# Joining two kinds of small-tile matmul runs, and one subtraction moved from VectorE to GpSimd

## The chip, the cores and the metric

The kernel runs on one core of a Trainium2 chip. The metric is the device time of one execution in microseconds (us). The profile is of one execution on the same chip; its span runs from its first instruction to its last.

## What is computed

The output is the sum of three things over a sequence of 2048 rows of 576 channels: the input itself, a long convolution (a diagonal state-space model, applied by FFT), and a feed-forward block. Both branches take the same layer-normalised input.

```python
def _A_ref(u, A_re, A_im, B_re, B_im, C_re, C_im, log_dt, Dskip):
    dt = jnp.exp(log_dt)[:, None]
    logdA, dB = dt * (A_re + 1j * A_im), dt * (B_re + 1j * B_im)
    P = jnp.exp(logdA[:, :, None] * l[None, None, :])        # l = 0..2047
    K = jnp.einsum("dn,dnl,dn->dl", C_re + 1j * C_im, P, dB).real
    ...
    Yf = rfft(u, padded) * rfft(K, padded)
    y = irfft(Yf)[:, :L] + u * Dskip
def _B_ref(x, w1, w2):
    return silu(x @ w1) @ w2                                 # 576 -> 4608 -> 576
xn = layernorm(A_u)
return A_u + _A_ref(xn, ...) + _B_ref(xn, w1, w2)
```

## The kernel before

**The main stream** is the feed-forward block (`ffn`, lines 257 to 446). It walks over 36 blocks: two halves of the rows, nine chunks of the hidden dimension, two row blocks of 512. `up` (L331 to L333) makes four 128 x 512 tiles `ph` of a chunk's hidden values, `down` (L357) multiplies them with the second weights into `po` tiles of 128 x 288, and VectorE adds each into the accumulator `acc` (L361). All matmuls are in a three-term form: every operand is split into a high and a low part (`gh`, `gl`, `w1h`, `w1l` and so on), ScalarE (ACT) making the high one and VectorE (DVE) the low one by a subtraction.

**The side stream** (`side`, from L863) is the convolution. The generator `weave` (L33) mixes it into the main stream: each `yield` of the side stream names a share of the main stream's steps, and the code up to the next `yield` is issued when the main stream has come that far. The last word on the order has a scheduler, which plans all engines' queues when the program is built; `tc.high_priority()` and `tc.issue_after` (here `behind(ins)`) are its hints. Each engine then runs its own queue strictly in that order. The stage from mark 0.13 to mark 0.597 of the main stream holds two parts:

- `kgen` (L584 to L728) makes the first transform of the convolution kernel K, 8 channels of each of two groups per step, 36 steps. A step makes tables `S` and `C` of 128 x 16 x 96 on DVE and ACT (L653 to L677). Every second step, after two steps' tables (a pair), 64 small matmuls of tile shape 128 x 32 write the response products `kp` (L696; the profile counts 128, since a float32 matmul runs in two passes). ACT copies them to `kt` (L703). Then eight small matmuls of tile shape 64 x 128 apply the first transform, into two PSUM tiles `z` (L711, counted as 16), and ACT copies those into `stage` (L719). Every second pair, two DMAs on SyncE's queue (SP) store `stage` into `d1k` (L724). Behind the loop, a GpSimd DMA adds the skip weights into `d1k` (L727).
- `spread` (L145 to L166) makes the first transform of the inputs, 16 row groups in two halves each, one half per step of `kgen`. A half loads `xr`, ACT casts its 64 rows to the high part in `sp` (L156), the low part is a subtraction of 64 x 576 (L157), four full-size matmuls make two `pu` tiles (L161, L162), ACT copies them to `u1` (L163), and a DMA on GpSimd's queue stores them to `d1u` (L164). The pool `up` has one buffer of each of `xr`, `sp` and `u1`.

`kp`, `z` and `pu` take their PSUM buffers from one pool, `pss`, with three. `po` takes from `ps2` (three), `ph` from `ps1` (two). Then the spectral stage (`spectral`, from L730) reads `d1u` and `d1k`, multiplies the spectra (`pk`, `pu`, `pb`, L826), and stores to `d2`; `add_conv` (L847, small tiles `py`) adds the inverse transform to the output rows.

Of the kernel before, what the change touches and what calls it, by code (L numbers as in the profile page):

```python
# [11 lines left out]
F32 = mybir.dt.float32  # L12
# [7 lines left out]
P = 128  # L20
# [23 lines left out]
def kernel(  # L44
# [21 lines left out]
    nc = tc.nc  # L66
# [14 lines left out]
    d1k = dram.tile([32 * P, D], F32, name="d1k")  # L81
# [9 lines left out]
    f1 = cst.tile([P, P], F32, name="f1")  # L91
# [18 lines left out]
    pss = ctx.enter_context(tc.tile_pool(name="pss", bufs=3, space=PSUM))  # L110
# [31 lines left out]
    def behind(ins):  # L142
        return tc.issue_after(ins) if ins is not None else nullcontext()

    def spread(up):  # L145

        s1 = up.tile([P, 2, P], F32R, name="s1", bufs=1)
        nc.gpsimd.dma_start(s1, cs1)
        for j in range(NJ):
            src = up.tile([P, D], F32, tag="xr", name="xr")  # L150
            nc.sync.dma_start(src, dxn[:, j])
            for m in range(2):
                lo, hi = slice(64 * m, 64 * m + 64), slice(64 - 64 * m, 128 - 64 * m)
                u1 = up.tile([P, D], F32, tag="u1", name="u1")
                sp = up.tile([P, D], F32R, tag="sp", name="sp")
                nc.scalar.copy(sp[lo, :], src[lo, :])  # L156
                nc.vector.tensor_sub(sp[hi, :], src[lo, :], sp[lo, :])  # L157
                for h in range(2):
                    hs = slice(h * HD, (h + 1) * HD)
                    pu = pss.tile([P, 512], F32, tag="pss", name="pu")  # L160
                    nc.tensor.matmul(pu[:, :HD], s1[:, 0, :], sp[:, hs], start=True, stop=False)  # L161
                    nc.tensor.matmul(pu[:, :HD], s1[:, 1, :], sp[:, hs], start=False, stop=True)  # L162
                    nc.scalar.copy(u1[:, hs], pu[:, :HD])  # L163
                nc.gpsimd.dma_start(  # L164
                    d1u.rearrange("(p m j) d -> m j p d", m=2, j=NJ)[m, j], u1)
                yield j  # L166
# [417 lines left out]
    def kgen():  # L584
        fT, phiT = kf["f"], kf["phi"]
        with tc.tile_pool(name="kg", bufs=1) as kg:
            CH = 8
            NRUN = 4
# [46 lines left out]
            def head(i):  # L635
                th = kg.tile([P, W, 65], F32, tag="th", name="th", bufs=2)
                nc.vector.tensor_mul(split(th), row(vt[:, 0:65], 65), col(fT, i, 65))
                with behind(pins["gl"]):
                    nc.vector.tensor_add(split(th)[:, :, :, :32], split(th)[:, :, :, :32], col(phiT, i, 32))
                return th  # L640

            stage = None
            tabs = []
            nxt = head(0)
            al = powers(0)
            for i in range(NCK):
                th = nxt
                pk, ak = pw[:, i % 2], al[:, :, i % 2]
                c65 = kg.tile([P, W, 65], F32, tag="c65", name="c65")
                S = kg.tile([P, W, 96], F32, tag="S", name="S", bufs=2)  # L650
                C = kg.tile([P, W, 96], F32, tag="C", name="C", bufs=2)
                mag = C
                nc.scalar.activation(c65, th, AF.Identity, bias=magic)  # L653
                nc.vector.scalar_tensor_tensor(th, c65, MAGIC, th, op0=ALU.subtract, op1=ALU.subtract)  # L654
                nc.scalar.activation(c65, th, AF.Abs)  # L655
                nc.scalar.activation(th, th, AF.Sin, scale=TWO_PI)
                nc.scalar.activation(c65, c65, AF.Sin, scale=-TWO_PI, bias=halfpi)
                for g in range(2):
                    gs = slice(g * CH, (g + 1) * CH)
                    nc.vector.tensor_mul(  # L660
                        mag[:, gs, 0:32].rearrange("n d (x y) -> n d x y", y=4),
                        pk[:, gs, 0, :].unsqueeze(3).broadcast_to([P, CH, 8, 4]),
                        ak[:, g].unsqueeze(2).broadcast_to([P, CH, 8, 4]))
                nc.vector.tensor_mul(
                    mag[:, :, 32:96].rearrange("n d (x y) -> n d x y", y=8),
                    pk[:, :, 1, :].unsqueeze(3).broadcast_to([P, W, 8, 8]),
                    pk[:, :, 2, :].unsqueeze(2).broadcast_to([P, W, 8, 8]))
                if i + 1 < NCK:
                    nxt = head(i + 1)
                    if i % 2 == 1:  # L670
                        al = powers(i + 1)
                for dst, t, sg in ((S, th, -1.0), (C, c65, 1.0)):
                    ov3 = dst.rearrange("n d (x y) -> n d x y", y=32)[:, :, 0:3:2, :]
                    mv3 = mag.rearrange("n d (x y) -> n d x y", y=32)[:, :, 0:3:2, :]
                    nc.vector.tensor_mul(ov3, t[:, :, 0:64].rearrange("n d (x y) -> n d x y", y=32), mv3)
                    nc.vector.scalar_tensor_tensor(dst[:, :, 32:64], t[:, :, 64:32:-1], sg, mag[:, :, 32:64],  # L676
                                                   op0=ALU.mult, op1=ALU.mult)  # L677
                tabs.append((S, C))
                if i % 2 == 0:
                    yield (i + 1) / NCK  # L680
                    continue

                kp = pss.tile([P, 512], F32, tag="pss", name="kp")
                first = None
                for e in (1, 0):
                    S, C = tabs[e]
                    for gl in range(2):
                        for gp_ in range(2):
                            o = e * 256 + (gl * 2 + gp_) * 64
                            for q in range(4):  # L690
                                ch = gp_ * CH + gl * 4 + q
                                dst = kp[32 * q:32 * q + 32, o:o + 64]
                                begins = e == 1 and gl == 0 and gp_ == 0
                                with tc.high_priority(), behind(None if begins else first):
                                    for n, t in enumerate((C, S)):
                                        mm = nc.tensor.matmul(dst, t[:, ch, :32], t[:, ch, 32:],  # L696
                                                              start=begins and n == 0, stop=True,
                                                              tile_position=(0, 32 * q), skip_group_check=True)
                                if begins:
                                    first = mm.ins  # L700
                tabs = []
                kt = kg.tile([P, 512], F32, tag="kt", name="kt")
                nc.scalar.copy(kt, kp)  # L703

                z = [pss.tile([P, 512], F32, tag="pss", name="z") for _ in range(2)]
                first = None
                for eg in range(4):
                    for h in (1, 0):
                        rows = slice(64 * h, 64 * h + 64)
                        with tc.high_priority(), behind(first):  # L710
                            mm = nc.tensor.matmul(z[h][:, eg * P:(eg + 1) * P], kt[rows, eg * P:(eg + 1) * P], f1[rows],  # L711
                                                  start=True, stop=True, tile_position=(64 * h, 0))
                        first = first or mm.ins
                r = (i - 1) % NRUN
                if r == 0:
                    stage = kg.tile([P, 64, NRUN * CH], F32, tag="stage", name="stage")
                sv = stage[:, :, r * CH:(r + 2) * CH].rearrange("p k (e h c) -> p h e k c", h=2, c=2)
                for h in range(2):
                    nc.scalar.copy(sv[:, h], z[h].rearrange("p (e k c) -> p e k c", e=4, c=2))  # L719
                if r == NRUN - 2:  # L720
                    d0 = (i // NRUN) * NRUN * CH
                    kv = d1k.rearrange("(k n) (g d) -> g n k d", n=64, g=2)
                    for gp_ in range(2):
                        nc.sync.dma_start(kv[gp_, :, :, d0:d0 + NRUN * CH], stage[gp_ * 64:(gp_ + 1) * 64])  # L724
                yield (i + 1) / NCK

        nc.gpsimd.dma_start(d1k.rearrange("(k n) d -> n k d", n=P)[0],  # L727
                            dskip.unsqueeze(0).broadcast_to([32, D]), accum_op=ALU.add)  # L728
# [294 lines left out]
```

## Time and profile before

| what | value |
|---|---|
| median of three runs | 1110.31 us (1109.8 to 1110.34) |
| span of the profiled execution | 1108.2 us |
| around the span, against the median | 2.1 us |
| TensorE busy in the span | 1102.2 us (99%) |
| VectorE busy in the span | 916.6 us (83%) |
| ScalarE busy in the span | 706.9 us (64%) |
| GpSimd busy in the span | 72.1 us (7%) |

The profile names engines PE (TensorE matmul), PEld (its weight loads), DVE (VectorE), ACT (ScalarE), POOL (GpSimd) and SP (SyncE). A row of the timeline has the start in us from the span's start, the duration in us, the engine, the line of the kernel, the operation, the tile written and those read, and the shape; "x4" merges four equal ones. A row of groups has the count, the busy time in us, the mean duration in ns, and the idle time ahead of the group with what ended it. A row of windows has the stretch, its length, each engine's busy time with its count of instructions, and at the end the granted clock of TensorE, the DMA engines' share and GB/s. Matmuls are pipelined: their durations overlap, so the distance from start to start is what one costs.

### The profile page before, as it was taken

Reading aid. Unit: us, or ns where it says so; the run is one execution under the profiler, and the core shown is the slowest. Engines: PE = TensorE matmul, PEld = TensorE weight load, DVE = VectorE, ACT = ScalarE, POOL = GpSimd, SP = SyncE. Lnnn points to the kernel's source line nnn. Section 1 sums busy time; section 2 is a strip of 40 time slices with the busy share of each in tenths; the row PEclk is TensorE's granted clock in tenths of the full one; section 3 lists DMA queues with packets and bytes.
Section 4 is the critical chain, followed back from the end, with each engine's and each line's share of the span. In section 5 each row is a group of like instructions: output and inputs, shape, how many; then the busy total and the mean of one; then the engine's idle time right before and its main releaser. Section 6 shows DMA issues by size and latency. Waiting matters only on the chain.

```text
span 1108.2 us, 22917 instructions
## 1 busy us (share of the span) xinstructions
PE 1102.2 (99%) x9167; PEld 997.5 (90%) x9167; DVE 916.6 (83%) x1543; ACT 706.9 (64%) x1222; POOL 72.1 (7%) x129
## 2 busy tenths in 40 slices
PE   9999999999999999999999999999999999999998
PEld 7989998899998899899999989999999999999887
DVE  7799899999999999999999737787778778784433
ACT  4564466676677676677867536877777878774210
POOL 1100000000000000011000000000000000000111
PEclk9999999999999999999999999999999999999999
DMA  9745512525252525264744173554544455434983
GB/s 270 190 123 160 152 50 61 120 73 131 77 121 83 116 72 118 77 174 154 206 122 103 45 179 109 162 167 123 156 145 152 138 149 170 129 107 127 241 224 87
DMA packets 175755, 148.56 MB, mean 134 GB/s; under 512 B 111088, under 2 KB 142592, under 8 KB 175520
## 3 DMA queue, kind: packets, MB, share of 16 engines
q1 hardware_dynamic: 165328, 112.63, 38.7%
q0 software_dynamic: 9568, 33.62, 9.6%
q8 instruction: 72, 1.18, 0.5%
q10 hardware_dynamic: 752, 0.85, 0.3%
q14 instruction: 35, 0.29, 0.1%
HBM read 102.53 MB, written 44.61 MB: 133 GB/s over the span
## 4 chain that ended last, share of the span: by engine, by line
PE 98%; DMA 1%; DVE 1%; SPq 0%; issue 0%; DVEq 0%
PE po L357 42%; PE ph L331 35%; PE kp L696 3%; PE ph L332 3%; PE ph L333 3%; PE pu L826 2%; PE pb L826 2%; PE pk L826 2%; PE z L711 2%; PE pu L161 1%; PE py L847 1%; DMA acc<-in_A_u_dram 1%; PE pu L162 1%; PE pt L124 0%; DVE w1l L295 0%; PE ptk L490 0%
## 5 line engine op out<-in xcount | busy, mean ns | idle before, releaser
L357 PE MATMUL po<-w2l,gh 128*128 128x288 f32 x1152 | 338.5, 295 | 0.0
L357 PE MATMUL po<-w2h,gl 128*128 128x288 f32 x1152 | 336.4, 295 | 0.0
L357 PE MATMUL po<-w2h,gh 128*128 128x288 f32 x1152 | 336.1, 295 | 0.0
L357 PEld LDWEIGHTS po<-w2h,gh 128*128 128x128 f32 x1152 | 215.2, 188 | 7.7 <-issue 2.8
L357 PEld LDWEIGHTS po<-w2l,gh 128*128 128x128 f32 x1152 | 215.9, 188 | 5.1 <-issue 0.5
L357 PEld LDWEIGHTS po<-w2h,gl 128*128 128x128 f32 x1152 | 215.4, 188 | 0.9
L339 ACT ACTIVATE gf<-ph 128x512 f32<-128x512 f32 (+1 forms) x148 | 86.4, 584 | 143.8 <-PE ph L333 134.8
L331 PE MATMUL ph<-xh,w1l 128*128 128x512 f32 (+1 forms) x592 | 161.3, 385 | 0.0
L331 PE MATMUL ph<-xh,w1h 128*128 128x512 f32 (+1 forms) x592 | 161.3, 387 | 0.0
L331 PE MATMUL ph<-xl,w1h 128*128 128x512 f32 (+1 forms) x592 | 161.1, 385 | 0.0
L361 DVE TENSOR_TENSOR acc<-po,acc 128x288 f32<-128x288 f32 x288 | 126.2, 451 | 37.0 <-PE po L357 35.6
L342 DVE TENSOR_TENSOR gl<-gf,gh 128x512 fp32r<-128x512 f32 (+1 forms) x148 | 99.0, 672 | 64.6 <-ACT gh L340 63.8
L331 PEld LDWEIGHTS ph<-xh,w1l 128*128 128x128 f32 x592 | 108.0, 188 | 20.0
L331 PEld LDWEIGHTS ph<-xl,w1h 128*128 128x128 f32 x592 | 107.9, 188 | 19.8
L331 PEld LDWEIGHTS ph<-xh,w1h 128*128 128x128 f32 x592 | 104.5, 188 | 16.7 <-ACT x L133 0.5
L340 ACT CAST gh<-gf 128x512 fp32r<-128x512 f32 (+1 forms) x148 | 89.5, 608 | 9.5 <-PE po L357 6.6
L653 ACT ACTIVATE c<-th,magic 128x1040 f32<-128x1040 f32 x36 | 42.1, 1168 | 37.9 <-DVE C L676 28.0
L655 ACT ACTIVATE c<-th 128x1040 f32<-128x1040 f32 x36 | 38.7, 1075 | 33.6 <-DVE th L654 33.6
L314 ACT CAST w2h<-w2r 128x576 fp32r<-128x576 f32 x72 | 47.0, 671 | 17.7 <-PE po L357 14.9
L295 DVE TENSOR_TENSOR w1l<-w1r,w1h 128x640 fp32r<-128x640 f32 x72 | 56.9, 817 | 0.2
L332 PE MATMUL ph<-x,w1h 128*128 128x512 f32 (+1 forms) x148 | 57.0, 386 | 0.0
L333 PE MATMUL ph<-x,w1l 128*128 128x512 f32 (+1 forms) x148 | 56.9, 385 | 0.0
(185 smaller groups left out, 1828.8 us busy)
## 6 DMA issues: line engine op xcount, KB each, us to landing
w2r<-in_B_w_dram SPq DMA_DIRECT2D x72, 288.0 KB, 3.8
w1r<-in_B_w_dram SPq DMA_DIRECT2D x35, 512.0 KB, 3.8
d1u<-u POOLq DMA_DIRECT2D x32, 288.0 KB, 2.5
d1k<-stage SPq DMA_DIRECT2D x18, 512.0 KB, 6.8
ur<-d1u SPq DMA_DIRECT2D x32, 288.0 KB, 3.7
kr<-d1k SPq DMA_DIRECT2D x32, 288.0 KB, 2.9
d<-yo POOLq DMA_DIRECT2D x32, 288.0 KB, 4.0
ys<-d SPq DMA_DIRECT2D x32, 288.0 KB, 11.8
```

The source lines that it names most:

```text
L295: pins["w1l"] = nc.vector.tensor_sub(l1, src, h1).ins
L314: pins["w2h"] = nc.scalar.copy(h2, r2).ins
L331: nc.tensor.matmul(ph, w[:, kt, :], v[:, kt, a:e], start=n + kt == 0, stop=False)
L332: nc.tensor.matmul(ph, h1[:, 4, :], x4[:, a:e], start=False, stop=False)
L333: pins["pe"] = nc.tensor.matmul(ph, l1[:, 4, :], x4[:, a:e], start=False, stop=True).ins
L339: nc.scalar.activation(gf, ph, AF.Silu)
L340: pins["gh"] = nc.scalar.copy(gh, gf).ins
L342: pins["gl"] = nc.vector.tensor_sub(gl, gf, gh).ins
L357: pins["pe"] = nc.tensor.matmul(po[:, :HD], G[blk, t][g][:, js], W2[half, c, t][w][:, hs], start=n == 0, stop=n == 3 * FT - 1).ins
L361: nc.vector.tensor_add(acc[j][:, hs], po[:, :HD], acc[j][:, hs])
L653: nc.scalar.activation(c65, th, AF.Identity, bias=magic)
L826: nc.tensor.matmul(dst, st, mv[:, hs], start=n == 0, stop=n == 3 * len(terms) - 1)
```

## The change

Two edits. The eight matmuls of the first transform of K, with what follows them (the ACT copies into `stage` and the store into `d1k`), become a function `turn`, which is called one pair late: the response products of a pair are issued, then `turn` for the pair before, whose first matmul is to stand behind the last response product. `kt` gets two buffers for that. The last pair's `turn` is called behind the loop. And the subtraction for the low part of `sp` is issued on GpSimd.

```diff
-                nc.vector.tensor_sub(sp[hi, :], src[lo, :], sp[lo, :])
+                nc.gpsimd.tensor_sub(sp[hi, :], src[lo, :], sp[lo, :])
...
+            stages = []
+            def turn(kt, i, first):
+                z = [pss.tile([P, 512], F32, tag="pss", name="z") for _ in range(2)]
+                for eg in range(4):
+                    for h in (1, 0):
+                        rows = slice(64 * h, 64 * h + 64)
+                        with tc.high_priority(), behind(first):
+                            mm = nc.tensor.matmul(z[h][:, eg * P:(eg + 1) * P], kt[rows, eg * P:(eg + 1) * P], f1[rows],
+                                                  start=True, stop=True, tile_position=(64 * h, 0))
+                        if eg + 1 - h == 0:
+                            first = mm.ins
...
+                for h in range(2):
+                    nc.scalar.copy(sv[:, h], z[h].rearrange("p (e k c) -> p e k c", e=4, c=2))
+                if r == NRUN - 2:
...
+                        nc.sync.dma_start(kv[gp_, :, :, d0:d0 + NRUN * CH], stage[gp_ * 64:(gp_ + 1) * 64])
...
+                                last = mm.ins
...
                 tabs = []
-                kt = kg.tile([P, 512], F32, tag="kt", name="kt")
+                if whole is not None:
+                    turn(*whole, last)
+                kt = kg.tile([P, 512], F32, tag="kt", name="kt", bufs=2)
                 nc.scalar.copy(kt, kp)
-                z = [pss.tile([P, 512], F32, tag="pss", name="z") for _ in range(2)]
...
+                whole = kt, i
                 yield (i + 1) / NCK
+            turn(*whole, None)
```

More of the change, by code (lines that the diff above doesn't have):

```diff
@@ L640, in head @@
                 return th
-            stage = None
+            stages = []
[9 more added lines that the diff above has]
+                            first = mm.ins
+                r = (i - 1) % NRUN
+                if r == 0:
+                    stages.append(kg.tile([P, 64, NRUN * CH], F32, tag="stage", name="stage"))
+                stage = stages[-1]
+                sv = stage[:, :, r * CH:(r + 2) * CH].rearrange("p k (e h c) -> p h e k c", h=2, c=2)
+                for h in range(2):
+                    nc.scalar.copy(sv[:, h], z[h].rearrange("p (e k c) -> p e k c", e=4, c=2))
+                if r == NRUN - 2:
+                    d0 = (i // NRUN) * NRUN * CH
+                    kv = d1k.rearrange("(k n) (g d) -> g n k d", n=64, g=2)
+                    for gp_ in range(2):
+                        nc.sync.dma_start(kv[gp_, :, :, d0:d0 + NRUN * CH], stage[gp_ * 64:(gp_ + 1) * 64])
+            whole = None
             tabs = []
@@ L683, in kgen @@
                 kp = pss.tile([P, 512], F32, tag="pss", name="kp")
-                first = None
+                last = None
                 for e in (1, 0):
@@ L701, in kgen @@
                 tabs = []
-                kt = kg.tile([P, 512], F32, tag="kt", name="kt")
+                if whole is not None:
+                    turn(*whole, last)
+                kt = kg.tile([P, 512], F32, tag="kt", name="kt", bufs=2)
                 nc.scalar.copy(kt, kp)
-                z = [pss.tile([P, 512], F32, tag="pss", name="z") for _ in range(2)]
[L706 to L724, printed above, removed]
+                whole = kt, i
                 yield (i + 1) / NCK
+            turn(*whole, None)
         nc.gpsimd.dma_start(d1k.rearrange("(k n) d -> n k d", n=P)[0],
```

## The prediction

> **What bounds the kernel now.** I read the page's engine sums first, then the chain that ended last, then the stage of the change by windows.
>
> ```profile
> span 1108.2 us, 22917 instructions
> PE 1102.2 (99%) x9167; PEld 997.5 (90%) x9167; DVE 916.6 (83%) x1543; ACT 706.9 (64%) x1222; POOL 72.1 (7%) x129
> PE 98%; DMA 1%; DVE 1%; SPq 0%; issue 0%; DVEq 0%
> ```
>
> The span is TensorE (PE) from end to end: 1102.2 of 1108.2 us busy, and 98% of the chain. So the time changes in two ways only: PE spends fewer or more nanoseconds on its own list, or it is made to wait. The list itself is the same in both programs (the built orders hold equal counts of every instruction; only 32 subtractions go from VectorE, DVE, to GpSimd, POOL). The span is one profiled execution; the median of the three timed runs is 1110.31 us, 2.1 us above it, and I carry differences from one to the other.
>
> Both parts of the change lie in the middle of the span, in the kernel and first-transform stage. There the second engine matters too:
>
> ```profile
> 160.00:610.00 450.00, 437.50 (x654) 1.00 0.42 111
> 200.00:300.00 100.00, 97.64 (x148) 1.00 0.39 102
> 300.00:400.00 100.00, 98.85 (x148) 1.00 0.40 101
> 400.00:500.00 100.00, 95.49 (x143) 1.00 0.44 115
> 500.00:600.00 100.00, 98.24 (x149) 1.00 0.52 143
> 160.00:610.00 450.00, 450.00 (x4694) 406.37 (x4694) 437.50 (x654) 315.49 (x477) 20.44 (x37) 1.00 0.42 111
> ```
>
> The first five rows are DVE's busy time in stretches of the stage, the last has PE, PEld, DVE, ACT, POOL. PE has no idle nanosecond in 450 us, at full granted clock (1.00), and DVE is idle only 12.5 us of them. PE is the bound, but DVE stands a step behind it, and POOL is empty.
>
> **Part 1: the runs of small tiles.** What PE pays at the border between full-size and small-tile matmuls is seen in start times (first number of a row, us), here of one response run's end (kp), then of one transform run's begin and end (z):
>
> ```profile
> 197.18 0.22 PE L696 MATMUL kp<-S 128*32 128x64 f32 x1
> 197.33 0.40 PE L357 MATMUL po<-w2l,gh 128*128 128x288 f32 x1
> 197.57 0.29 PE L357 MATMUL po<-w2h,gl 128*128 128x288 f32 x1
> 197.70 0.29 PE L357 MATMUL po<-w2h,gh 128*128 128x288 f32 x1
> ...
> 202.58 0.39 PE L332 MATMUL ph<-x,w1h 128*128 128x512 f32 x1
> 202.81 0.39 PE L333 MATMUL ph<-x,w1l 128*128 128x512 f32 x1
> 203.13 0.38 PE L711 MATMUL z<-f,kt 64*128 64x128 f32 x2
> ...
> 204.01 0.27 PE L711 MATMUL z<-f,kt 64*128 64x128 f32 x1
> 204.22 0.40 PE L161 MATMUL pu<-sp,s 128*128 128x288 f32 x1
> 204.46 0.30 PE L162 MATMUL pu<-sp,s 128*128 128x288 f32 x1
> 204.59 0.39 PE L331 MATMUL ph<-xh,w1h 128*128 128x512 f32 x1
> ```
>
> Two full-size matmuls follow each other after 0.13 us (288 columns: 197.57 to 197.70) or 0.23 us (512 columns: 202.58 to 202.81). Going into z, the 512-column one is followed after 0.32 us: 0.09 extra. Coming out of kp, 0.15 us pass, where small ones follow each other after about 0.01; then the first full-size one takes 0.24 in place of 0.13: 0.11 extra, a weight load that hides behind no matmul. Out of z it is the same, 0.21 us and then 0.24.
>
> Before: 18 kp runs and 18 z runs, each alone. In the built order of the changed program 17 z runs stand directly behind the next pair's kp run, the first kp run stands alone, and the last pair's z run, which has no later kp, is cut into two halves with full-size matmuls between. A merge takes away one stretch of full-size work between two small ones: 0.11 (first full-size matmul) + 0.09 (entry to z) = 0.20 us, if the step from kp to z costs what the step out of kp costs (0.15). 17 x 0.20 = 3.4 us. The cut last run adds one more entry and exit: 0.09 into it, 0.11 for a first small weight load in the open (I take it like the full-size one), 0.10 extra out of it, 0.11 for the full-size one behind it: 0.4 us. Sum: **3.0 us less**.
>
> No row of before shows a step from kp tiles (128x32) to z tiles (64x128). Bounds: at worst it costs the whole round trip through full size, and the merge saves nothing (0); at best it costs nothing, saving also the 0.14 of kp's exit and z's 0.11 weight load, 0.25 x 17 = 4.2 us more. I take the middle, since both rows of a change of tile shape (in and out) show the pipe emptied first.
>
> The Trainium skill (TensorEngine Tiling (Array Packing), Tiling Modes, Key Properties) says that a change of tiling mode drains the array and a change of tile alone does not. The rows above agree at the border to full size (0.09 and 0.15 us); kp to z is by that page a change of mode, so by the rule the sum stays 3.0 us, and without a drain it would be 7.2.
>
> What the moved z drags along: its two evictions on ACT and the d1k stores on SP come one pair later, for all pairs but the last. Nothing reads d1k before the spectral stage, and the last z run keeps its distance: by the slots above, the first spectral product stands some 34 us of PE work behind it in the new order, 32 in the old. A merged run needs three PSUM buffers of the ring of three at once (kp and two z). Ahead of it, the ring's former users, the pu products of the first transform, stand at least 6.0 us of PE work away, so the buffers are free. Behind it they are nearer than the gap may seem: the next pu stands 2.3 us or more after the z run's start, and takes the buffer that the kt copy frees, the second pu one of z's:
>
> ```profile
> L719 ACT COPY stage<-z 128x512 f32<-128x512 f32 x36 | 21.3, 651 | 7.3 <-PE z L711 7.3
> L703 ACT COPY kt<-kp 128x512 f32<-128x512 f32 x18 | 10.3, 574 | 15.2 <-PE kp L696 15.2
> ```
>
> With ACT free, kt is copied 0.6 us after kp's end and the first z 0.65 us after z's end (0.9 after its start): 1.6 of 2.3 us. I cost this at nothing; where ACT comes a microsecond late, PE stands still for about 0.65 us (an eviction), up to 17 times.
>
> **Part 2: the subtraction on POOL.**
>
> ```profile
> L157 DVE TENSOR_TENSOR sp<-xr,sp 64x576 fp32r<-64x576 f32 x31 | 23.3, 753 | 1.0
> L198 POOL TENSOR_TENSOR sd<-sd,mhalf 128x2 f32<-128x2 f32 (+1 forms) x9 | 8.2, 910 | 94.6 <-DVE sd L197 94.6
> L464 POOL TENSOR_TENSOR e<-e,dt 96x6 f32<-96x6 f32 x1 | 1.7, 1732 | 0.0
> 5.33 0.57 POOL L198 TENSOR_TENSOR sd<-sd,mhalf 128x1 f32<-128x1 f32 x1 [2.31 <-DVE sd L197]
> ```
>
> DVE loses 31 x 0.753 = 23.3 us in the window 160 to 610: 437.5 becomes 414.2 of 450. That alone moves no time, since PE never waits there. POOL's price is not in the trace: its tensor operations are tiny. The nearest rows are 0.57 us for one column (nearly all fixed cost) and 1.73 for the longest; with DVE's own 0.75 for this shape as the streaming part, 0.57 + 0.75 = 1.3 us is my estimate, bounds 0.75 to 1.73. The GPSIMD Engine Reference of the Trainium skill (section 3.1) gives 2.6 cycles an element, an estimate of 1.25 us for 576.
>
> Does the wait that this adds reach PE? The pu matmuls now wait for POOL. The chain from a freed sp buffer is the ACT cast (0.67), a DVE operation in POOL's way (1.23, next fence) and 1.3 on POOL: 3.2 us, or 5.5 with two of ACT's longer instructions (1.17) ahead. The least PE work between one half's last pu and the next half's first is 6.1 us in the new order. So it is hidden, with 0.6 us to spare. Behind the subtraction on POOL stands only that half's store of d1u (0.54 us to issue), which waits for ACT in any case, and d1u is read by the spectral stage alone.
>
> ```profile
> L156 ACT CAST sp<-xr x31: 667/672/692, 180.4 to 605.4; 64x576 fp32r<-64x576 f32 x31
> L653 ACT ACTIVATE c<-th,magic 128x1040 f32<-128x1040 f32 x36 | 42.1, 1168 | 37.9 <-DVE C L676 28.0
> 377.79 1.23 DVE L637 TENSOR_TENSOR th<-vt,fT 128x1040 f32<-128x1040 f32 x1
> ...
> 80.52 0.95 DVE L531 TENSOR_TENSOR t<-t 96x768 f32<-96x768 f32 x1
> 81.39 0.68 DVE L342 TENSOR_TENSOR gl<-gf,gh 128x512 fp32r<-128x512 f32 x1
> 80.76 1.27 POOL L198 TENSOR_TENSOR sd<-sd,mhalf 128x2 f32<-128x2 f32 x1 [20.89 <-DVE sd L197]
> ```
>
> The last three rows show the doubt: POOL's operation, 0.57 us alone, began at 80.76 beside a DVE product of two SBUF tiles, and ended at 82.03, 0.56 us after that product's end (81.47). So the two share something, and the one that came second stood still. In turn, the DVE operation at 81.39 ran its usual 0.68 us inside POOL's last 0.56: a two-column read holds DVE up by nothing visible. For 576 columns the hold h on DVE is bounded by 0 and by POOL's whole operation (1.3, at most 1.73). I take POOL's streaming part, 0.75, the nearest row: then DVE gets back what it lost, 437.5 again, and PE waits no more than now. DVE becomes the bound from h = (450 - 414.2) / 31 = 1.16 us on.
>
> The Trainium skill (SBUF — State Buffer, Who interferes with whom) calls this an exclusive lock, held for the whole instruction, between a GpSimd operation that reads SBUF and a DVE one with two SBUF inputs. The rows agree that POOL waits; that the hold lasts the whole instruction they contradict for two columns. By the rule h would be 1.25 and DVE 414.2 + 38.8 = 453.0 of 450.
>
> Sum: 1108.2 - 3.0 = 1105.2 for the span, **1107.3** on the median's scale.
>
> **The rivals.** (a) *DVE becomes the bound (slower).* h is POOL's whole 1.3 us. Net load per half 1.3 - 0.75 = 0.55, and 6.9 halves per 100 us: +3.8. The four 100-us rows come to 101.4, 102.6, 99.3 and 102.0; idle time of one stretch doesn't repay another, so PE waits 1.4 + 2.6 + 2.0 = 6.0 us: 1110.3 + 6.0 - 3.0 = 1113.3. At 1.73 it is +6.8 a row, 17.2 us, 1124.5. For it: POOL's wait above, and DVE's load. Against: the unlengthened 0.68 us, and matmuls from PSUM operands (acc, L361) that need no second SBUF read. It decides above h = 1.16.
>
> (b) *No drain between the tile shapes:* 1110.3 - 7.2 = 1103.1. For it: both are small shapes. Against: the pipe is emptied at each change that before shows.
>
> (c) *The merge's gain is given back on PE:* kp to z costs the round trip, or the pu behind the run waits for ACT's three copies, where five of 17 waits of 0.65 us give back 3.2: 1110.5. For it: 1.6 of 2.3 us with ACT free, and ACT's single instructions of 1.17; against: no such wait in before, where a pu stands directly behind 17 z runs.
>
> **How the numbers follow.** About 0.2% (2.2 us) is what a measurement of this kernel can tell from no change. Forecast 0.56 (1105.5 to 1108.5 as its own range, of which a small part, 0.05, is within 0.2%), (a) 0.25, (b) 0.08, (c) 0.11. Faster: 0.51 + 0.08 = 0.59. Same: 0.05 + 0.11 + 0.01 of (a) = 0.17. Slower: 0.24. The range leaves out (b)'s far end and (a)'s upper third: 1104 to 1115.
>
> **What would show it.** Right: a kp row followed by a z row after about 0.15 us; 17 merged runs; PE with no idle time on pu, kp or po from 160 to 610; DVE's busy time near 437 there, or less; POOL rows of L157 near 1.3 us. Wrong: DVE products beside POOL's rows at 2 us and more, DVE at 450 of 450 and PE waiting on acc, C or S (rival a); z behind kp after 0.01 us (b); PE waiting on ACT inside a run (c), or on POOL ahead of pu, which would break the 0.6 us of spare.

## The result, and the profile after

The changed kernel takes **1128.45 us** (median of 4 runs, 1126.68 to 1133.5), the kernel before 1110.32 us beside it: the ratio is **1.017, 95% interval 1.0151 to 1.0189**. It is slower by 18.1 us; 1107.3 had been forecast, in a range of 1104 to 1115. The profiled execution is the slowest of the four, 1133.5 us with a span of 1131.7; the mildest has a span of 1124.9.

First the page of the changed kernel: span, engine sums, and the shares of the chain that ended last.

```profile
span 1131.7 us, 22934 instructions
PE 1110.7 (98%) x9167; PEld 1003.8 (89%) x9167; DVE 915.4 (81%) x1511; ACT 705.4 (62%) x1222; POOL 145.5 (13%) x161
PE 56%; DVE 20%; issue 13%; ACT 4%; DMA 4%; POOL 2%; SPq 0%; DVEq 0%; ACTq 0%; POOLq 0%
```

PE held 98% of the chain before, and now holds 56%. DVE's sum is what it was (915.4 against 916.6), although 32 subtractions have left it: the rest of its list has become longer by as much. Now the stage of the change (windows: stretch, length, then PE, PEld, DVE, ACT, POOL, and at the end the granted clock, the DMA share and GB/s):

```profile
160.00:610.00 450.00, 437.62 (x4566) 393.47 (x4565) 417.68 (x598) 301.00 (x458) 86.36 (x64) 0.99 0.40 105
```

PE, without an idle nanosecond here before, now idles 12.4 us and gets through 128 matmuls fewer. DVE is not full either: 417.7 of 450. What PE waits for, in the view of waits (total us, times, longest):

```profile
PE pu L161 <- ACT kt L732: 6.2, 5, 1.9
PE py L857 <- DMA ys<-d: 2.6, 1, 2.6
PE pu L161 <- POOL sp L157: 2.3, 2, 1.9
PE pu L161 <- ACT stage L661: 1.8, 2, 1.5
```

Most of it stands at `pu`, the product that the prediction named as the place of two risks: kt's copy on ACT (L732 here), and the subtraction on POOL (L157). Of that subtraction the view of groups and the view of the tile (ns min/median/max) show:

```profile
L157 POOL TENSOR_TENSOR sp<-xr,sp 64x576 fp32r<-64x576 f32 x32 | 72.8, 2274 | 23.2 <-ACT sp L156 21.3
...
L157 POOL TENSOR_TENSOR sp<-xr,sp x32: 1417/1944/4541, 138.0 to 619.8; 64x576 fp32r<-64x576 f32 x32
```

Left alone it takes 1.42 us, at the median 1.94, at worst 4.54. Three places of the timeline show what it meets (DVE's rows and POOL's of the same stretch):

```profile
328.58 0.69 DVE L702 SCALAR_TENSOR_TENSOR C<-c,C 128x512 f32<-128x512 f32 x1
329.18 2.46 DVE L637 TENSOR_TENSOR th<-vt,fT 128x1040 f32<-128x1040 f32 x1
328.72 1.82 POOL L157 TENSOR_TENSOR sp<-xr,sp 64x576 fp32r<-64x576 f32 x1
...
381.43 1.22 DVE L701 TENSOR_TENSOR C<-c,C 128x1024 f32<-128x1024 f32 x1
382.57 1.93 DVE L702 SCALAR_TENSOR_TENSOR C<-c,C 128x512 f32<-128x512 f32 x1
382.21 1.73 POOL L157 TENSOR_TENSOR sp<-xr,sp 64x576 fp32r<-64x576 f32 x1
...
516.50 1.23 DVE L637 TENSOR_TENSOR th<-vt,fT 128x1040 f32<-128x1040 f32 x1
517.66 0.68 DVE L342 TENSOR_TENSOR gl<-gf,gh 128x512 fp32r<-128x512 f32 x1
518.26 0.68 DVE L639 TENSOR_TENSOR th<-th,phiT 128x512 f32<-128x512 f32 x1
518.86 1.28 DVE L382 TENSOR_TENSOR xl<-xl,xh 128x512 fp32r<-128x512 f32 x2
520.07 0.45 DVE L361 TENSOR_TENSOR acc<-po,acc 128x288 f32<-128x288 f32 x1
520.43 1.33 DVE L631 TENSOR_TENSOR pw<-pw 128x192 f32<-128x192 f32 x1
517.06 4.34 POOL L157 TENSOR_TENSOR sp<-xr,sp 64x576 fp32r<-64x576 f32 x1
```

At 329.18 and at 382.57 a DVE product that takes 1.23 and 0.68 us elsewhere takes 1.23 and 1.25 longer: it makes next to no headway until POOL's operation is over (330.54, 383.94). At 517 it goes the other way first: products of two SBUF tiles follow each other without a gap, and POOL shows no headway for 3 us. It gets in beside `acc`, which reads PSUM, from 520.07; at 520.43 pw (0.51 us before) starts, is held for the rest, 0.83, and POOL ends at 521.40. So the two exclude each other, a whole hold is 1.24 us, and it is shorter where POOL has begun beside an `acc` or a gap. Over the 32 operations DVE is lengthened by 23.5 us (each DVE instruction beside POOL's, less the median of its kind): 0.73 us a subtraction.

What PE makes of the place at 517:

```profile
519.18 0.40 PE L331 MATMUL ph<-xh,w1l 128*128 128x512 f32 x1
521.46 0.42 PE L161 MATMUL pu<-sp,s 128*128 128x288 f32 x1 [1.88 <-POOL sp L157]
```

It stands for 1.88 us until POOL's result is there. And the merged run itself:

```profile
357.59 0.22 PE L722 MATMUL kp<-C 128*32 128x64 f32 x1
357.61 0.31 PE L722 MATMUL kp<-S 128*32 128x64 f32 x6
357.85 1.16 PE L651 MATMUL z<-f,kt 64*128 64x128 f32 x16
358.94 0.40 PE L357 MATMUL po<-w2h,gh 128*128 128x288 f32 x1
359.18 0.30 PE L357 MATMUL po<-w2l,gh 128*128 128x288 f32 x1
```

The last six kp products start about 0.02 us apart from 357.61, so z starts 0.15 us after the last of them, and behind it the first full-size product takes 0.24: the prices of the forecast. In all 17 merged runs that step lies between 0.149 and 0.150 us.

### The profile page after: what moved, and what is told of

Read it like the earlier page. It is cut to its first block, busy times and chain, and to the rows that moved or that the text cites. A ratio compares the mean times of both kernels' runs of the same rounds, so it can differ in the third digit from the quotient of the medians.

```text
span 1131.7 us, 22934 instructions
## 1 busy us (share of the span) xinstructions
PE 1110.7 (98%) x9167; PEld 1003.8 (89%) x9167; DVE 915.4 (81%) x1511; ACT 705.4 (62%) x1222; POOL 145.5 (13%) x161
## 4 chain that ended last, share of the span: by engine, by line
PE 56%; DVE 20%; issue 13%; ACT 4%; DMA 4%; POOL 2%; SPq 0%; DVEq 0%; ACTq 0%; POOLq 0%
PE po L357 24%; PE ph L331 20%; PE pu L836 2%; PE pk L836 2%; PE pb L836 2%; DVE C L690 2%; DVE th L637 2%; DVE S L701 2%; DVE gl L342 2%; DVE th L680 2%; PE ph L333 2%; POOL sp L157 2%; PE ph L332 2%; DVE acc L361 2%; DVE w1l L295 2%
## 5 line engine op out<-in xcount | busy, mean ns | idle before, releaser
L342 DVE TENSOR_TENSOR gl<-gf,gh 128x512 fp32r<-128x512 f32 (+1 forms) x148 | 104.5, 710 | 62.3 <-ACT gh L340 62.0
L157 POOL TENSOR_TENSOR sp<-xr,sp 64x576 fp32r<-64x576 f32 x32 | 72.8, 2274 | 23.2 <-ACT sp L156 21.3
L679 ACT ACTIVATE c<-th,magic 128x1040 f32<-128x1040 f32 x36 | 41.9, 1165 | 52.5 <-DVE C L702 34.1
L681 ACT ACTIVATE c<-th 128x1040 f32<-128x1040 f32 x36 | 38.7, 1075 | 56.4 <-DVE th L680 56.3
L164 POOL DMA_DIRECT2D d1u<-u x32 | 17.9, 560 | 376.2 <-ACT u L163 337.8
L295 DVE TENSOR_TENSOR w1l<-w1r,w1h 128x640 fp32r<-128x640 f32 x72 | 59.4, 847 | 2.6 <-ACT w1h L293 2.3
## 6 DMA issues: line engine op xcount, KB each, us to landing
ys<-d SPq DMA_DIRECT2D x32, 288.0 KB, 11.5
```

Source lines behind the costliest of these rows:

```text
L157: nc.gpsimd.tensor_sub(sp[hi, :], src[lo, :], sp[lo, :])
L295: pins["w1l"] = nc.vector.tensor_sub(l1, src, h1).ins
L342: pins["gl"] = nc.vector.tensor_sub(gl, gf, gh).ins
```

## The experiments

**Theory:** GpSimd's reading of SBUF holds DVE's products (those with two inputs in SBUF) one at a time, PE is late wherever a held product feeds it, and this makes nearly all of the loss. **Rivals:** the merged run is at fault (kt's copy, the PSUM ring); the new order that the build makes, or `pu` waiting on another engine, is at fault rather than any hold; DVE's load as a whole is what counts, so that holds cost nothing until DVE is full.

### Each part alone

`e1_merge_only`, the changed kernel with one line undone:

```diff
-                nc.gpsimd.tensor_sub(sp[hi, :], src[lo, :], sp[lo, :])
+                nc.vector.tensor_sub(sp[hi, :], src[lo, :], sp[lo, :])
```

> Runs merged as in the changed kernel, the subtraction (L157) left on VectorE. Theory A (the GpSimd subtraction and VectorE's products hold each other up; VectorE's lateness passes through ScalarE's queue to the kt and stage copies, for which PE then waits ahead of pu): no PE wait ahead of pu, 17 steps from kp to z of 0.15 us, about 1107.3 us, 0.997 of before. Theory B (the merged run alone is at fault, since a pu stands 2.3 us behind it and needs the kt and stage copies): PE waits of 1 to 2 us ahead of several pu, about 1120 us.

`e2_pool_only`, the kernel before with this line alone changed, the other way round.

> The kernel before with the subtraction (L157) on GpSimd, runs not merged. Theory A: GpSimd rows of L157 near 1.9 us, VectorE products stretched beside them, PE waits in the stage, over 1120 us. Theory B: the GpSimd rows are as long, but PE doesn't wait, about 1110 us. If both parts are needed for the loss (the lateness from GpSimd and the pu close behind the run), 1110 to 1114 us.

Measured: e1 1115.72 us against 1110.64, ratio 1.0046 (1.0034 to 1.0059); e2 1134.48, ratio 1.0216 (1.0202 to 1.0229). **Both parts lose.** POOL's part alone loses 23.8 us, more than the whole change; the merge alone loses 5.1 where 3.0 was to be gained. Together they lose 18.1, so the two don't add; why the changed kernel loses less than e2 stays open. e1 lies between its two expectations. The windows of e1, then of e2, in the same stretch:

```profile
160.00:610.00 450.00, 445.49 (x4657) 403.87 (x4657) 433.60 (x648) 311.15 (x472) 20.47 (x37) 1.00 0.41 109
```

```profile
160.00:610.00 450.00, 437.24 (x4553) 389.47 (x4552) 417.76 (x594) 297.59 (x452) 82.36 (x64) 1.00 0.39 105
```

e2 shows the stage of the changed kernel over again, PE idle for 12.8 us and DVE idle for 32, without any merged run. So the merge isn't the main cause.

### A hold without a new order

e2's order differs from before's, so a rival is left. Four kernels keep the kernel before with its subtraction on DVE, and add one operation on GpSimd whose result nobody reads. The order on PE, DVE and ACT is the same as before's, instruction by instruction; no other engine waits for the addition. Only the next load of `xr`, whose buffer the addition reads, comes behind it, and ACT waits no longer for that load in e3 than before (2.8 us against 2.9). `e3_extra_sub`:

```diff
                 nc.vector.tensor_sub(sp[hi, :], src[lo, :], sp[lo, :])
+                junk = up.tile([P, D], F32, tag="junk", name="junk")
+                nc.gpsimd.tensor_sub(junk[lo, :], src[lo, :], src[lo, :])
```

> The kernel before, with 32 additional subtractions of 64x576 on GpSimd whose result nobody reads (xr minus xr into a tile of its own); VectorE keeps its own subtraction, and the order on PE, VectorE and ScalarE is that of before. Theory A, holding: VectorE's busy time in the stage rises by 0.6 us or so per subtraction, about 20 us in all, from 437.5 of 450 to beyond 450, and PE loses some 10 to 20 us: 1120 to 1130 us. If the holding of VectorE is no cause by itself (only that pu waits for GpSimd's long operation): 1110 us.

`e4_extra_set` writes as much and reads nothing:

```diff
-                nc.gpsimd.tensor_sub(junk[lo, :], src[lo, :], src[lo, :])
+                nc.gpsimd.memset(junk[lo, :], 0.0)
```

> As the run before, but the 32 additional GpSimd operations write zeros and read nothing (memset of 64x576), with the same order on PE, VectorE and ScalarE. Theory A, with the holding on the read side: VectorE's rows stay at their lengths and the time at 1110.3 us. If any GpSimd operation of that length holds VectorE up: slower like the extra subtractions.

`e5_extra_sub_half` subtracts half of the columns (`junk[lo, :HD]`, `src[lo, :HD]`), and `e6_extra_copy` reads one input over all 576 (`nc.gpsimd.tensor_copy(junk[lo, :], src[lo, :])`).

> The extra GpSimd subtractions again, nobody reading them, with 288 in place of 576 columns; the order on PE, VectorE and ScalarE is that of before. In the run with 576 columns 28 of 32 stretched one VectorE operation each, by up to 0.98 us, 22.8 us in all, and the time rose by 25.8. Hold theory: a hold is as long as GpSimd reads, so about 0.48 us here and 11 to 12 us in all. Every unplanned us of VectorE costs PE one (no threshold): about 1123 us. VectorE only costs time once it is the bound (437.5 of 450 busy before, so up to 12.5 us are free): 1110 to 1111 us.

> The extra GpSimd operation reads one input (copy of 64x576) in place of two. If the hold is GpSimd's reading, 0.48 us per operation as in the run with 288 columns of two inputs, and the same time (1123 us without a threshold, 1111 us with one). If only a two-input operation holds VectorE: 1110.3 us.

| run | median us | ratio (95%) | DVE busy in the span | GpSimd operation, least ns |
|---|---|---|---|---|
| before | 1110.64, 1110.47 | | 916.6 | |
| e3, 576 columns, two inputs | 1136.42 | 1.0238 (1.0224 to 1.0252) | 939.8 | 1137 |
| e4, 576 columns, no input | 1110.3 | 0.9999 (0.999 to 1.0009) | 916.4 | 572 |
| e5, 288 columns, two inputs | 1122.27 | 1.0108 (1.0091 to 1.0125) | 927.2 | 657 |
| e6, 576 columns, one input | 1122.03 | 1.0104 (1.0089 to 1.0119) | 927.1 | 664 |

The view of groups of e3, by shape in 160 to 610, and below it the same group of e4:

```profile
L662 DVE TENSOR_TENSOR C<-pw,wb 128x256 f32<-128x256 f32 x60 | 30.1, 541 | 0.6 <-PE kp L698 0.6
```

```profile
L662 DVE TENSOR_TENSOR C<-pw,wb 128x256 f32<-128x256 f32 x64 | 24.0, 416 | 0.0
```

And e3's timeline at one place, where two of these products meet two subtractions:

```profile
225.75 2.66 DVE L662 TENSOR_TENSOR C<-pw,wb 128x256 f32<-128x256 f32 x2
225.12 3.00 POOL L159 TENSOR_TENSOR junk<-xr 64x576 f32<-64x576 f32 x2 [6.82 <-DMA xr<-dxn]
```

Two products of 0.42 us take 2.66 together. With the order kept, each DVE instruction of e3 can be set against the same one of before: 28 of the 32 subtractions lengthen one, usually by 0.95 us, never by more than 0.98. In e5 the greatest is 0.49, in e6 0.47; in e4 none is longer by 0.1. So a whole hold is POOL's own least duration less 0.16 to 0.19 us (1.137 to 0.95, 0.657 to 0.49, 0.664 to 0.47, and in the changed kernel 1.417 to 1.24): it lasts about as long as POOL works alone, whether it reads one input or two. Twice the columns hold twice as long (usually 0.47 us in e5, 0.95 in e3), so the hold goes with the columns read, and the rest of POOL's duration holds nobody. By that two columns would hold for some 0.003 us, an estimate from e3 and e5, which fits the unlengthened row at 81.39 in the prediction. Writing alone holds nothing: e4's fills ran early, from 132 to 152 us, but beside DVE operations throughout, and the fills of e11 and e12 below, which are spread from 132 to 602 us, lengthen DVE's operations by 0.2 us in all or less. Nor is `acc`, which reads PSUM, held: 19 of them ran beside an addition in e3, and none is longer by 0.01 us.

The price falls out too. 23.2 us of lengthening cost 26.4 us (0.0238 x 1110), 10.6 cost 12.0 and 10.5 cost 11.5: **1.1 us of time for each us of hold**, with no free part at the start. Half clock on TensorE (last section) is a part of it, some 5.1 us in e3's profiled execution; but executions of e5 and e6 at a mean clock of 1.000 still lost 11.4 and 11.0 us. In e5 DVE would still have been inside its 450 us (437.5 + 10.6). So the rival that DVE's load decides, with a threshold, is refuted.

### Both parts without the reading

`e11_pool_set` is e2, and `e12_after_set` the changed kernel, with GpSimd writing zeros in place of subtracting. DVE stays relieved; the low part of the input's first transform is left out.

```diff
-                nc.gpsimd.tensor_sub(sp[hi, :], src[lo, :], sp[lo, :])
+                nc.gpsimd.memset(sp[hi, :].bitcast(F32), 0.0)
```

> The kernel of run e2 (before, with only the subtraction for sp moved to GpSimd), but GpSimd writes zeros in place of subtracting: the low part of the input's first transform is left out, so the output isn't the reference's. PE's list of matmuls is the same in number and shapes; VectorE stays relieved of 32 x 0.753 = 24.1 us; GpSimd reads nothing for sp. Theory (what costs is GpSimd's reading, which holds VectorE's two-input operations, about 1.1 us of PE for each us of hold): no DVE operation stretched, PE waits back near zero, 1108 to 1114. Rival (what costs in e2 is the new order that the relief and the move bring, or that pu now waits on another engine): as in e2, 1128 to 1136.

> The changed kernel, but GpSimd writes zeros in place of subtracting: the low part of the input's first transform is left out, so the output isn't the reference's. Merged runs stay. Theory (holds cost +23 or so, merging +5 by its waits): 1110 to 1117, the merge's waits of about 5 us remain, no DVE operation stretched. Rival (order or the wait on another engine): 1124 to 1132. If VectorE's relief of 24 us also takes away the merge's waits for kt: below 1110.

Measured: e11 1111.35 us against 1110.64, ratio 1.001 (1.0 to 1.002); e12 1110.12, ratio 0.9997 (0.9987 to 1.0007). A line of e11's page, then page and window of e12:

```profile
PE 1102.6 (99%) x9167; PEld 998.3 (90%) x9167; DVE 891.7 (80%) x1511; ACT 708.1 (64%) x1222; POOL 90.4 (8%) x161
...
PE 1100.1 (99%) x9167; PEld 998.7 (90%) x9167; DVE 891.7 (80%) x1511; ACT 705.4 (64%) x1222; POOL 90.4 (8%) x161
...
160.00:610.00 450.00, 449.86 (x4819) 408.59 (x4818) 416.32 (x629) 316.52 (x478) 38.26 (x68) 1.00 0.40 109
```

`pu` still needs GpSimd's result here, and the order is again a new one; yet PE is full, and 23 us (e2) and 18 us (changed kernel) are gone. GpSimd doesn't wait for the ACT cast in these two, and their order isn't e2's or the changed kernel's, so they take away an operand's wait along with the reading; e3, with no such wait and no new order, shows the reading alone to cost as much. DVE's sums tell it in one row each: 916.6 before, 891.7 relieved, 915.4 in the changed kernel, relieved and held. Without merged runs the relief is worth nothing, since PE waited for nobody (e11 against before). The holds cost 23.1 us in e2 against e11, and 18.3 in the changed kernel against e12, for 26.2 and 23.7 us more of DVE time: 0.9 and 0.8 us for each us of hold in these orders, where the extra operations above cost 1.1.

e12 didn't come out as its theory had it: the merge's waits of about 5 us were to remain, and none for kt is left. So beside merged runs the relief does count, e12 being 5.6 us below e1; but its order is another than e1's, and the two causes aren't separated.

e12 also shows the merge when nothing is in its way. PE's work is 1100.1 us, 2.5 less than e11's 1102.6 without it, near the 3.0 forecast; such a sum is good to about 1 us, since e4, with before's list and order, has 1101.1 where before has 1102.2. The median is lower by only 1.2, since PE then stands at the first load of the inverse transform (`add_conv`):

```profile
PE py L857 <- DMA ys<-d: 1.7, 1, 1.7
```

### Where the merge loses its gain

PE's waits in e1, and the timeline of ACT and of PE at one of them:

```profile
PE pu L161 <- ACT kt L732: 3.2, 4, 1.1
PE po L357 <- ACT w2h L314: 1.1, 2, 0.6
PE ph L331 <- ACT gf L339: 1.0, 1, 1.0
...
385.70 1.16 ACT L679 ACTIVATE c<-th,magic 128x1040 f32<-128x1040 f32 x1 [1.85 <-DVE th L639]
386.77 0.60 ACT L340 CAST gh<-gf 128x512 fp32r<-128x512 f32 x1
387.27 1.35 ACT L293 CAST w1h<-w1r 128x640 fp32r<-128x640 f32 x2
388.53 1.06 ACT L681 ACTIVATE c<-th 128x1040 f32<-128x1040 f32 x1
389.50 0.56 ACT L732 COPY kt<-kp 128x512 f32<-128x512 f32 x1
...
385.59 1.16 PE L651 MATMUL z<-f,kt 64*128 64x128 f32 x16
386.68 0.40 PE L357 MATMUL po<-w2h,gh 128*128 128x288 f32 x1
...
390.12 0.40 PE L161 MATMUL pu<-sp,s 128*128 128x288 f32 x1 [1.04 <-ACT kt L732]
```

The last kp product starts ahead of 385.59, and its copy could follow at once, but it stands behind five other ACT operations, two of which (L679, L681) take what DVE makes. The copy frees kp's PSUM buffer, and the next `pu` takes it. The kernel before had such late copies too, as at this place:

```profile
223.78 0.31 PE L696 MATMUL kp<-S 128*32 128x64 f32 x6
228.14 0.58 ACT L703 COPY kt<-kp 128x512 f32<-128x512 f32 x1
232.44 1.16 PE L711 MATMUL z<-f,kt 64*128 64x128 f32 x16
```

Over the 18 runs of before the copy ended 2.1 us behind kp's end on the mean and 4.6 at most, but the z run stood at least 3.3 us behind kp, and the next `pu` at least 4.4, so nobody waited. In e1 it ends 2.8 us behind on the mean, and the next `pu` may stand only 2.3 us behind: the margin has gone, and the copy has become a little later. Four kernels try to mend this.

`e7_merge_ps2` takes `pu` from the other PSUM ring, `e8_merge_late` holds `pu` back in PE's order, `e9_merge_even` issues two halves of the inputs' first transform at every second step of `kgen` in place of one at each, and `e10_merge_abs` keeps the copy ahead of the next Abs on ACT. Each is e1 with:

```diff
-                    pu = pss.tile([P, 512], F32, tag="pss", name="pu")
+                    pu = ps2.tile([P, 512], F32, tag="ps2", name="pu")
```

```diff
-                    nc.tensor.matmul(pu[:, :HD], s1[:, 0, :], sp[:, hs], start=True, stop=False)
+                    with behind(pins["pe"]):
+                        nc.tensor.matmul(pu[:, :HD], s1[:, 0, :], sp[:, hs], start=True, stop=False)
```

```diff
-                    if n > 1:
+                    if n > 1 and n % 2 == 0:
+                        next(sp, None)
                         next(sp, None)
```

```diff
-                nc.scalar.activation(c65, th, AF.Abs)
+                with behind(pins.get("kt") if i % 2 == 0 else None):
+                    nc.scalar.activation(c65, th, AF.Abs)
...
-                nc.scalar.copy(kt, kp)
+                pins["kt"] = nc.scalar.copy(kt, kp).ins
```

> Merged runs, subtraction on VectorE, and the pu tiles of the first transform take their PSUM buffers from the pool of po (ps2) in place of the one of kp and z. If merging alone lost time because pu waits for the kt copy to free its buffer: the waits of PE ahead of pu for kt (3.9 us in the merge-only run) go, and the time falls below before, to 1107 to 1109 us. If the merge is slow for another reason: 1115 us again.

> Merged runs, subtraction on VectorE, and each pu asked to stand behind the last feed-forward matmul issued before it; in the built order the least distance from a z run's start to the next pu is still 2.3 us, as in the merge-only run. If the wait for kt is the cause: some of it stays, 1112 to 1116 us. If it is not: 1115 to 1116 us.

> Merged runs, subtraction on VectorE, and both halves of the input transform issued in the steps without a response run. In the built order the first pu stands 3.1 us or more behind a z run's start (4.3 on the mean; 2.3 and 3.5 in the merge-only run). If the merge-only run lost time because pu waits for the late kt copy: those waits go or shrink, and the time falls to or below before, 1107 to 1110 us. If not: 1115 us.

> Merged runs, subtraction on VectorE, and ScalarE's Abs of every second step (L681) asked to stand behind the kt copy, so that this copy no longer waits in ScalarE's queue for VectorE's th; the first pu still stands 2.3 us or more behind a z run's start. If ScalarE's order is what makes the kt copy late: no wait ahead of pu for kt, 1107 to 1109 us, unless the later Abs makes VectorE's tables late, in which case PE waits at kp and the time stays at or over 1112 us.

| run | median us | ratio (95%) | PE's largest waits, us |
|---|---|---|---|
| e1 | 1115.72 | 1.0046 (1.0034 to 1.0059) | pu for kt 3.2, po for w2h 1.1, ph for gf 1.0 |
| e7 | 1133.92 | 1.0212 (1.0197 to 1.0227) | pu for acc 3.2, ph for w1h 3.0, for gf 2.9, po for u 2.7 |
| e8 | 1118.66 | 1.007 (1.0055 to 1.0085) | pu for kt 4.0, py for its load 2.4 |
| e9 | 1118.68 | 1.0078 (1.0064 to 1.0092) | po for w2h 3.2, py for its load 1.8 |
| e10 | 1114.49 | 1.0041 (1.0028 to 1.0054) | po for gl 1.6, py for its load 0.9 |

e10's waits have no row with kt of 0.3 us or more:

```profile
PE po L357 <- DVE gl L342: 1.6, 1, 1.6
...
PE py L858 <- DMA ys<-d: 0.9, 1, 0.9
```

So ACT's order made kt late: pinning the copy ahead of one operation ends those waits. But the time hardly falls, since `po` waits for `gl` and others wait in their place. e7 ends kt's waits too, but the users of the other ring wait (`pu` for acc, `po` for u, 5.9 us), and `ph` waits for ACT besides (5.9). e8 tells little: its `pu` stands no farther behind z than in e1 (3.5 us of PE work on the mean against 3.7), and the waits for kt stay. e9 loses kt's waits but for 0.2 us, and pays at `po`. All three came out slower than either of their expectations. That the merge's small gain is lost to the new order, at whichever place is tight in it, fits all of them, but is argued. None of these versions beats the kernel before.

## Why the prediction was wrong

**What bounds the kernel.** Right, but read too far. PE had no idle time, and DVE 12.5 us in 450. I took DVE's 437.5 as a sum that may be moved about as long as it stays below 450.

**Part 1, the merge, 3.0 us.** The price of the step was right (0.15 us in all 17 runs), and PE's list did become some 2.5 us shorter where nothing covers it (e12 against e11). The rival without a drain (1103.1) is refuted by the same step. The Trainium skill (TensorEngine Tiling (Array Packing), Tiling Modes, Key Properties) has a change of tiling mode drain the array; the 0.15 us from kp to z agree.

**What the moved z drags along, at nothing.** This failed, by e1. I checked that PSUM buffers are free "with ACT free", and ACT wasn't: in the trace of before, 12 of the 18 kt copies begin over 1 us behind kp's end. That did no harm while z and `pu` stood farther off, and does with 2.3 us of margin. Rival (c) named just this, 0.65 us at a time, and 1110.5; it is 1115.7 alone, with 3.2 us of waits for kt, and 2.1 more for w2h and gf from ACT. In the changed kernel the waits for kt and stage make 8.0 us, the largest item among PE's waits.

**Part 2, POOL's price and its chain.** 1.3 us was the estimate, and 1.42 is the least. But 1.94 is the median, as DVE keeps POOL out in turn, up to 4.5 us in all. "Hidden, with 0.6 us to spare" fails there: PE waits for it twice, 2.3 us in all.

**The hold h.** 0.75 was taken, a mean of 0.73 was measured, and the forecast that DVE "gets back what it lost" came true, 915.4 against 916.6 us in the span. That was luck. The hold is POOL's streaming part, as I had it, but that part isn't DVE's 0.75: a whole hold is 1.24 us, and the mean is smaller only because some of POOL's time falls beside `acc` or a gap. The Trainium skill (GPSIMD Engine Reference, section 3.1) gives 2.6 cycles an element for a two-input operation, which is the estimate of 1.25 us for 576. The 1.24 agrees, but e3's subtraction with as many columns, of `xr` from itself into plain float32, holds for 0.95; which of these differences makes it was not tried. The Trainium skill (SBUF — State Buffer, Who interferes with whom) speaks of an exclusive lock for the whole instruction, between GpSimd and two-input DVE operations. I set it against a two-column row and thought it contradicted; with 576 columns the runs agree with it, but for some 0.18 us of POOL's duration.

**"and PE waits no more than now".** This is the step that failed, and it is worth some 23 us (e2 against e11). It took time that DVE gives up and time that DVE is held as the same, and equal sums are not equal times: DVE's subtraction was in the order before, its 24 us under PE's cover, so taking them away gives nothing where PE waits for nobody (e11). The holds are as many us at places where a product or a copy is due (`gl`, w1l, th and, through ACT, c and kt), and they cost 1.1 times their length in before's order (e3, e5, e6), 0.8 to 0.9 in the new ones. Why the rate is so near one is only argued: PE is fully used and the order fixed, so what is late at a due place isn't made up by DVE's idle time elsewhere.

**Rival (a), DVE as the bound, 1113.3 to 1124.5.** Its sign was right, and so was its single hold (1.3 against 1.24). Its mechanism wasn't: DVE was busy 417.7 of 450 us, and the threshold of 1.16 us doesn't exist. A range built on that threshold ended at 1115; and that end leaves out some four fifths of the rival's span from 1113.3 to 1124.5, not its upper third. Of the marks named, DVE's products at 2 us and more beside POOL's rows did appear (2.46 at 329.18), and PE's waits on ACT behind a run; DVE at 450 didn't.

## What to carry to other kernels

An operation on GpSimd that reads SBUF is not free work beside a VectorE full of two-input SBUF products: count about its least duration as a hold on whichever product it meets, at nearly full price where TensorE is the bound, and count nothing for VectorE's relief as long as TensorE waits for nobody. Where a step is moved, read from the trace how late the copies behind it already are, and ask who else waits for what they free: a copy that comes 2 to 4 us late without harm becomes a wait once the next user of its PSUM buffer stands 2.3 us away. Test such a doubt with an extra operation whose result nobody reads: here it kept the order, and priced the contention by itself.

## What the hardware showed besides

After most waits of about 2 us or more TensorE ran at half clock for 3.4 us. The windows of the changed kernel around the wait that ended at 419.01 (the clock is the third number from the end):

```profile
418.90:419.30 0.40, 0.29 (x2) 0.32 (x3) 0.40 (x1) 0.40 (x2) 0.00 (x0) 0.99 0.00 0
419.30:422.70 3.40, 3.40 (x16) 3.40 (x15) 3.40 (x6) 0.88 (x3) 0.00 (x0) 0.50 0.21 53
422.70:423.10 0.40, 0.40 (x5) 0.40 (x4) 0.40 (x1) 0.36 (x2) 0.00 (x0) 1.00 1.04 366
```

This happened four times in the profiled execution, each time behind a wait of 1.8 to 2.6 us, and not behind the two of 1.5 us. The length of the wait doesn't settle it: over all profiled runs 13 of the 17 waits of 1.8 to 3.1 us came with such a stretch, and four didn't (2.1 us in e3, 2.4 in e8, 1.8 and 2.2 in e9); none of 1.7 us or less did. Half the clock for 3.4 us loses 1.7 us, 6.8 in all, about what sets this execution (span 1131.7 at a mean clock of 0.994) apart from the one with full clock (1124.9 at 1.000). It adds to the loss, and doesn't make it.

GpSimd can be starved as well: in e3 the subtraction that began at 264.07 took 7.96 us in place of 1.14. DVE ran a dozen operations beside it, most of them products of two SBUF tiles, with no gap between them.
